# Scores of a decode attention: K transposed on TensorE in place of products on VectorE, and longer loads

## The chip, the cores and the metric

One core of a Trainium2 chip runs the whole kernel as one program. The metric is the time of one execution in microseconds on the device, as the median of several runs. Engines are named as in the profile: PE (TensorE matmuls), PEld (TensorE weight loads), DVE (VectorE), ACT (ScalarE), POOL (GpSimd) and SP (SyncE, which here issues the loads).

## The reference

Everything is float32. Two rows (B = 2 batches, one position each) of width 512 go through a layernorm; its result feeds an attention over a cache and a gated feed-forward, and both are added to the input.

```python
W = min(4096, max(256, Sk // 4))                      # 8192 // 4 = 2048 last positions
q = (xn @ wq).reshape(B, 1, 32, 128)                  # 32 heads of 128
scores = einsum("bhqd,bhkd->bhqk", q, k_cache[:, :, Sk-W:]) * 128 ** -0.5
p = softmax(scores)
A = einsum("bhqk,bhkd->bhqd", p, v_cache[:, :, Sk-W:]) @ wo
g, u = xn @ w_gate, xn @ w_up                         # 512 x 1376 each
out = x + A + (g * u) @ w_down
```

For each of 64 (batch, head) pairs 2048 rows of K and as many of V are read once: 134.2 MB of the 159.6 MB that the kernel reads. Each query is one row, so there is no reuse.

## The kernel before

The host lays all inputs but x out as one DRAM stream, in the order in which they are loaded; each load is one block of 128 rows, one row a partition (`laid_out`, `loads`, `placed`). A ring of three SBUF tiles, all named `step` in the profile, takes the loads; a load reuses a place once its readers are done. All loads go out on SP's queue in program order (`issue`).

The 32 heads are worked in NG = 8 groups of HG = 4. K and V of a head are 128 partitions x 4096 floats (16 KB a row): the first 64 partitions hold batch 0, the others batch 1, and each partition has 32 positions of 128 values. A turn of the main loop (`for it in range(NG + 2)`) handles K of group `it` and V of group `it - 1`. Its loads are `{g}.0` (K of two heads, V of one), `{g}.1` (K of one, V of two) and `{g}.2` (wo, V of one, K of one, the next wq), mostly 6144 KB each with 48 KB rows.

- `project`: four matmuls with the normalized x, spread over 128 columns, leave the group's queries in PSUM tile `q`, each batch on its own 64 partitions.
- `products` and `sums`, per head: DVE multiplies K in place by the query (tile `step`) and adds up each 128 products (tile `s`). Both pass over 128x4096 elements.
- `maxima`, `spread`, `weights`, `denominators`: the group's maximum over all positions (DVE, a 32x32 transpose and a matmul with ones, tile `top`), subtraction, exp on ACT into `p`, and the sums `rs`, summed over partitions by a matmul into `tot`.
- `weigh`, per head: eight matmuls, each with 32 columns of `p` as weights and 512 columns of V as moving data, in four column groups of the array, into `o_ps`.
- `gather`, `scaled`, `wo`: ACT copies `o_ps` to SBUF, four small matmuls pick each head's 128 values, DVE scales them, and four matmuls with wo add to PSUM tile `acc`.

Gate and up (`project_gu`) run once in the first turn as 24 matmuls in three column groups into two PSUM tiles; `gate_up` multiplies them and transposes the product with small matmuls. The feed-forward's w_down comes in strips of 128 rows: four early (EARLY), the others at the end (ROWS into `acc`, STRIPS into the same tile as the final sum).

DVE, ACT, POOL and SP run straight code; PE runs a loop over named sections (`steer`, `pr.part`, with `pr.hold` for waits against a register that counts turns). `Program.put` finds the dependences, `plan` and `emit` turn them into semaphore waits. Every operation is recorded by one helper, so nearly all lines of the profile say L139, and groups are told apart by tile names.

Of the kernel before, what the change touches and what calls it, by code (L numbers as in the profile page):

```python
# [5 lines left out]
ALU = mybir.AluOpType  # L6
# [7 lines left out]
HB = P // B  # L14
J = W // HB
JG = J // 4
NC = D // P
FB = 4 * P
NFB = -(-F // FB)
# [8 lines left out]
CK, CO, CQ = J * DH, D, HG * DH  # L28
CX = B * NC + 4 * N + 4 * HG + 2 * NFB + 2 + B
EARLY, ROWS, STRIPS = (0, 5, 6, NFC), (1, 2, 3, 4), (7, 8, 9)  # L30
GU = [(w, c, n) for w in range(2) for c in range(NC) for n in range(NFB)]
GU_A = [(0, c, n) for c in range(NC) for n in (2, 0)] + [(0, 0, 1)]
GU_B = [t for t in GU if t not in GU_A]


def gu_cols(n):
    return min(FB, F - n * FB)


WIDTHS = {"k": CK, "v": CK, "wo": CO, "wd": CO, "wq": FB, "c": CX}  # L40

PLACES = {
    ("k", 0): (0, 0), ("k", 1): (0, CK), ("v", 0): (0, 2 * CK),
    ("k", 2): (1, 0), ("v", 1): (1, CK), ("v", 2): (1, 2 * CK),
    ("wo", 0): (2, 0), ("v", 3): (2, HG * CO), ("k", 3): (2, HG * CO + CK),
    ("wq", 0): (2, HG * CO + 2 * CK),
}
C_WQ = HG * CO + 2 * CK  # L50
C_C = C_WQ + NC * FB
TILES = (3 * CK, 3 * CK, C_C + CX)


def field_at(kind, i):
    if kind == "wq":
        return PLACES["wq", 0][0], C_WQ + i[1] * FB
    if kind == "wo":
        return 2, i % HG * CO
    if kind == "c":  # L60
        return 2, C_C
    return PLACES[kind, i % HG]


def loads():


    def k(*ids):
        return [("k", h) for h in ids]

    def v(*ids):
        return [("v", h) for h in ids]

    def wq(g):
        return [("wq", (g, c)) for c in range(NC)]

    def wo(g):
        return [("wo", h) for h in range(g * HG, g * HG + HG)]

    gu_a, gu_b = [("gu", t) for t in GU_A], [("gu", t) for t in GU_B]  # L80
    wd = {i: ("wd", i) for i in range(NFC + 1)}
    out = {
        "x": ("B2", wq(0) + [("c", 0)]),
        "0.0": ("B0", k(0, 1) + gu_a),
        "0.1": ("B1", k(2) + gu_b),
        "0.2": ("B2", [wd[i] for i in EARLY] + k(3) + wq(1)),
    }
    for g in range(1, NG):
        a, b = g * HG, g * HG - HG
        out[f"{g}.0"] = ("B0", k(a, a + 1) + v(b))  # L90
        out[f"{g}.1"] = ("B1", k(a + 2) + v(b + 1, b + 2))
        out[f"{g}.2"] = (
            "B2", wo(g - 1) + v(b + 3) + k(a + 3) + (wq(g + 1) if g + 1 < NG else [])
        )
    b = H - HG
    out[f"{NG}.0"] = ("B0", v(b))
    out[f"{NG}.1"] = ("B1", v(b + 1, b + 2))
    out[f"{NG}.2"] = ("B2", v(b + 3))
    out["wo"] = (None, wo(NG - 1))
    for name, ids in (("d0", ROWS), ("d1", STRIPS[:-1]), ("d2", STRIPS[-1:])):  # L100
        out[name] = (None, [wd[i] for i in ids])
    return out


def placed():


    got, spans = {}, {}
    for name, (_, fields) in loads().items():
        at, lo, tile = None, None, None  # L110
        for kind, i in fields:
            w = gu_cols(i[2]) if kind == "gu" else WIDTHS[kind]
            if kind == "gu":
                t, c = tile, at
            elif kind == "wd":
                if at is not None:
                    t, c = tile, at
                elif name == "0.2":
                    t, c = 2, HG * CO + CK - len(EARLY) * CO
                else:  # L120
                    t, c = 0, (ROWS + STRIPS).index(i) * CO
            else:
                t, c = field_at(kind, i)
            assert at is None or (t, c) == (tile, at), (name, kind, i, c, at)
            got[kind, i] = (t, c, w)
            lo = c if lo is None else lo
            tile, at = t, c + w
        assert at <= TILES[tile], (name, at)
        spans[name] = (tile, lo, at)
    return got, spans  # L130


class Op:
    def __init__(self, eng, method, args, kw, deps, dma, tag, place, holds):
        self.eng, self.method, self.args, self.kw = eng, method, args, kw
        self.deps, self.dma, self.tag, self.place, self.holds = deps, dma, tag, place, holds

    def call(self, engine):
        return getattr(engine, self.method)(*self.args, **self.kw)  # L139

    def same(self, other):
        def flat(x):
            if hasattr(x, "space"):
                return x.tensor.name, x.offset, [list(t) for t in x.ap]
            return x

        def all_of(o):
            return [o.method] + [flat(a) for a in o.args] + [
                (k, flat(a)) for k, a in sorted(o.kw.items())
            ]  # L150

        return all_of(self) == all_of(other)


class Program:


    def __init__(self, nc):
# [5 lines left out]
        self.tag, self.also, self.held = None, [], []  # L164
# [24 lines left out]
    def put(self, eng, method, writes, reads, args, kw, dma=False):  # L189
# [29 lines left out]
        self.ops.append(Op(eng, method, args, kw, deps, dma, tag, place, holds))  # L219
# [10 lines left out]
    def plan(self, looped):  # L230
# [15 lines left out]
        for i, o in enumerate(ops):  # L246
# [20 lines left out]
            if o.dma and o.tag in self.tags:  # L267
                prev = [j for j in self.tags[o.tag] if j < i]
                assert all(know.get(("dma", j)) for j in prev), (o.tag, i)
# [7 lines left out]
        for i, o in enumerate(ops):  # L277
            if o.dma:
# [8 lines left out]
    def emit(self, looped, control):  # L287
# [10 lines left out]
        def give(i, first=None):  # L298
# [5 lines left out]
            for s, v in w[:-1]:  # L304
                e.wait_ge(s, v)
            ins = o.call(e)
            if w:
                ins._wait_ge(*w[-1])
            if i in at:
                ins.then_inc(sem[o.tag], 16 if o.dma else 1)  # L310
# [86 lines left out]
def steer(prog, regs, run):  # L397
    nc, pe = prog.nc, prog.eng["PE"]
    only = [mybir.EngineType.PE]
    r, r16 = pe.alloc_register("turn"), pe.alloc_register("landed")  # L400
    regs.update(r=r, r16=r16)
    run("start")
    pe.reg_mov(r, 1)
    pe.reg_mov(r16, 16)
    pe.br("pe_top")
    with nc.body("pe_top", valid_engines=only):
        here = pe.mark_branch_hint_location()
        pe.br_lt(r, 3, on_true="pe_q", on_false="pe_g")
    with nc.body("pe_g", valid_engines=only):
        run("g")  # L410
        pe.br_lt(r, NG + 2, on_true="pe_q", on_false="pe_o")
    with nc.body("pe_q", valid_engines=only):
        run("q")
        pe.br_lt(r, 2, on_true="pe_gu", on_false="pe_t")
    with nc.body("pe_t", valid_engines=only):
        run("t")
        pe.br_lt(r, 3, on_true="pe_w", on_false="pe_o")
    with nc.body("pe_o", valid_engines=only):
        run("o")
        pe.br_lt(r, NG + 2, on_true="pe_w", on_false="pe_tail")  # L420
    with nc.body("pe_w", valid_engines=only):
        n = 3 * JG + 1
        run("w", 0, n)
        pe.reg_add(r16, r16, 16)
        run("w", n)
        pe.reg_add(r, r, 1)
        pe.br_lt(r, 2 * NG + 9, on_true="pe_top", on_false="pe_tail").branch_hint(here)
# [3 lines left out]
    with nc.body("pe_gu", valid_engines=only):  # L431
        run("gu")
        pe.reg_add(r, r, 1)
        pe.reg_add(r16, r16, 16)
        pe.br("pe_top")


def build(nc, stream, x_nat, out):
# [3 lines left out]
    ring = [pr.sb(f"step{i}", [P, w]) for i, w in enumerate(TILES)]  # L442
    xr = pr.sb("xr", [P, D])
    ones = pr.sb("ones", [P, P])
    mean_w = pr.sb("mean_w", [P, P])
    eps_t = pr.sb("eps", [P, 1])
    zero = pr.sb("zero", [P, 1])
    st = pr.sb("st", [P, 4, B])
    xc = pr.sb("xc", [P, 2, B, NC])
    xn = pr.sb("xn", [P, NC, B])  # L450
    xnb = pr.sb("xnb", [P, NC, P])
    p_all = pr.sb("p", [P, HG, JG, M])
    s_t = [pr.sb(f"s{i}", [P, HG, J]) for i in range(2)]
    mt = pr.sb("mt", [P, 32])
    mtt = pr.sb("mtt", [P, 32])
    mc = pr.sb("mc", [P, 1])
    dg = pr.sb("dg", [P, 4 * HG])
    rs = pr.sb("rs", [P, N])
    nm = pr.sb("nm", [P, HG])
    rec = pr.sb("rec", [P, N])  # L460
    oT = pr.sb("oT", [P, N])
    o_sb = pr.sb("o_sb", [P, FB])
    h_sb = pr.sb("h_sb", [P, FB])
    hT = pr.sb("hT", [P, 4, NFB, B])
    acc_sb = pr.sb("acc_sb", [P, D])
    o_out = pr.sb("o_out", [P, P])

    o_ps = pr.ps("o_ps", [P, FB])
    q_ps = pr.ps("q", [P, FB])
    acc = pr.ps("acc", [P, FB])  # L470
    top_ps = pr.ps("top", [P, FB])
    gu_ps = [pr.ps(f"gu{i}", [P, FB]) for i in range(2)]
    tot_ps = pr.ps("tot", [P, FB])
    hT_ps, pk_ps = gu_ps
    acc_g = q_ps[:, 0:P]

    where, spans = placed()
    got = {key: ring[t][:, c : c + w] for key, (t, c, w) in where.items()}
    src, pos, tag_of = {}, 0, {}
    for name, (tag, _) in loads().items():  # L480
        t, lo, hi = spans[name]
# [4 lines left out]
    def issue(name):  # L486
        t, lo, hi = spans[name]
        pr.load("SP", ring[t][:, lo:hi], src[name], tag=tag_of[name])

    issue("x")  # L490
    issue("0.0")
    issue("0.1")
    for t, v in ((mean_w, 1.0 / D), (eps_t, EPS), (ones, 1.0), (p_all, 0.0),
                 (xr, 0.0), (zero, 0.0), (mt, 0.0)):
        pool.memset(t, v)
    pr.load("ACT", xr[:B, :], x_nat)

    cst = got["c", 0]
    cut = [0]
# [341 lines left out]
```

## Time and profile before

| | |
|---|---|
| median of 3 runs | 376.31 us (376.18 to 377.29) |
| profiled execution | 375.96 us, its span 374.6 us |
| moved by DMA | 159.62 MB in 4756 packets, 426 GB/s over the span |
| load queue busy | 98.9% of the span |
| busy: DVE, PE, ACT, POOL | 299.5, 177.2, 18.3, 3.0 us |
| mean granted PE clock | 0.718 of full speed |

The profile is of one execution. Its span runs from the first to the last instruction. Rows of engines give busy tenths in 40 slices of the span; the DMA row gives the mean busy share of the 16 DMA engines. A row of the timeline has the start, the duration, the engine, the source line, the operation with its output and inputs, and in brackets how long the engine had been idle and what released it. A float32 matmul is two instructions, so "x8" is four matmuls. In a table by stretches, each engine has its busy time and its instructions; PEclk is the granted clock.

### The profile page before, as it was taken

Reading aid. Unit: us, or ns where it says so; the run is one execution under the profiler, and the core shown is the slowest. Engines: PE = TensorE matmul, PEld = TensorE weight load, DVE = VectorE, ACT = ScalarE, POOL = GpSimd, SP = SyncE. Lnnn points to the kernel's source line nnn. Section 1 sums busy time; section 2 is a strip of 40 time slices with the busy share of each in tenths; the row PEclk is TensorE's granted clock in tenths of the full one; section 3 lists DMA queues with packets and bytes.
Section 4 is the critical chain, followed back from the end, with each engine's and each line's share of the span. In section 5 each row is a group of like instructions: output and inputs, shape, how many; then the busy total and the mean of one; then the engine's idle time right before and its main releaser. Section 6 shows DMA issues by size and latency. Waiting matters only on the chain.

```text
span 374.6 us, 2080 instructions
## 1 busy us (share of the span) xinstructions
PE 177.2 (47%) x850; PEld 54.9 (15%) x850; DVE 299.5 (80%) x151; ACT 18.3 (5%) x42; POOL 3.0 (1%) x16
## 2 busy tenths in 40 slices
PE   0664743337516184073923277061740645334876
PEld 0210121002101030010400032010300112010322
DVE  0089999998599796997699975997969976999911
ACT  4000200000000000000000000000000000000000
POOL 3000000000000000000000000000000000000000
PEclk9965859587855688565695858567965659656899
DMA  9999999999999999999999999999999999989996
GB/s 365 415 457 408 444 420 420 457 467 420 420 420 420 430 493 420 420 420 420 425 462 457 420 420 420 420 441 483 420 420 420 420 425 472 446 382 431 439 411 275
DMA packets 4756, 159.62 MB, mean 426 GB/s; under 512 B 530, under 2 KB 658, under 8 KB 916
## 3 DMA queue, kind: packets, MB, share of 16 engines
q1 hardware_dynamic: 4752, 159.62, 98.9%
q10 hardware_dynamic: 4, 0.00, 0.0%
HBM read 159.55 MB, written 0.07 MB: 426 GB/s over the span
## 4 chain that ended last, share of the span: by engine, by line
DMA 50%; DVE 47%; PE 2%; issue 0%; SPq 0%; DVEq 0%
DMA step<-in_stream_dram 50%; DVE step L139 23%; DVE s L139 22%; PE q L139 2%; DVE rs L139 1%; SPq L139 0%; PE acc L139 0%; DVE h_sb L139 0%; PE top L139 0%; DVE nm L139 0%; DVE o_out L139 0%; DVE mt L139 0%; DVE dg L139 0%; DVE mtt L139 0%; DVE mc L139 0%
## 5 line engine op out<-in xcount | busy, mean ns | idle before, releaser
L139 DVE TENSOR_TENSOR step<-step,q 128x4096 f32<-128x4096 f32 x32 | 141.3, 4416 | 41.2 <-DMA step<-in_stream_dram 41.2
L139 PE MATMUL o_ps<-step,p 128*32 128x512 f32 x512 | 93.7, 884 | 156.2 <-DMA step<-in_stream_dram 153.7
L139 DVE TENSOR_REDUCE s<-step 128x32 f32<-128x4096 f32 x32 | 141.4, 4418 | 0.8
L139 PEld LDWEIGHTS o_ps<-step,p 128*32 128x32 f32 x512 | 18.7, 147 | 218.4 <-DMA step<-in_stream_dram 170.6
L139 PE MATMUL q<-step,xnb 128*128 128x512 f32 x72 | 42.0, 736 | 9.0 <-DVE step L139 6.3
L139 PEld LDWEIGHTS q<-step,xnb 128*128 128x128 f32 x72 | 16.5, 241 | 28.2 <-issue 18.2
L139 PE MATMUL gu<-step,xn 128*2 128x512 f32 (+1 forms) x48 | 14.8, 786 | 11.4 <-DMA step<-in_stream_dram 11.4
L139 ACT COPY o_sb<-o_ps 128x256 f32<-128x256 f32 x16 | 5.2, 375 | 247.3 <-PE o_ps L139 247.3
L139 PE MATMUL gu<-step,o_sb 128*128 128x8 f32 x64 | 10.1, 285 | 4.0 <-ACT o_sb L139 4.0
L139 PEld LDWEIGHTS gu<-step,o_sb 128*128 128x128 f32 x64 | 9.4, 225 | 16.5 <-ACT o_sb L139 16.5
L139 ACT ACTIVATE p<-s,zero 64x128 f32<-64x128 f32 x16 | 6.4, 399 | 63.5 <-DVE s L139 63.4
L139 PE MATMUL acc<-step,oT 128*2 128x512 f32 x64 | 8.3, 592 | 0.4 <-DVE oT L139 0.4
L139 DVE TENSOR_REDUCE nm<-top 64x4 f32<-64x8 f32 x16 | 2.6, 164 | 7.0 <-PE top L139 6.9
L139 DVE RECIPROCAL rec<-tot 128x8 f32<-128x8 f32 x8 | 1.6, 199 | 6.2 <-PE tot L139 6.2
L139 PEld LDWEIGHTS gu<-step,xn 128*2 128x2 f32 x48 | 2.9, 99 | 23.2 <-DMA step<-in_stream_dram 13.1
L139 PE MATMUL top<-dg,ones 128*128 128x16 f32 x16 | 2.9, 258 | 6.6 <-DVE dg L139 6.6
L139 DVE TENSOR_REDUCE st<-xc 128x4 f32<-128x16 f32 x1 | 0.2, 169 | 6.2 <-POOL xc L139 6.2
L139 DVE TENSOR_TENSOR oT<-gu,rec 128x8 f32<-128x8 f32 x8 | 1.3, 157 | 4.3 <-PE gu L139 4.3
L139 PEld LDWEIGHTS top<-dg,ones 128*128 128x128 f32 x16 | 2.5, 188 | 12.5 <-DVE dg L139 11.4
L139 DVE TENSOR_REDUCE rs<-p 128x8 f32<-128x256 f32 x8 | 3.3, 414 | 0.9 <-ACT p L139 0.9
L139 ACT ACT_TABLE_LOAD x3 | 3.8, 1283 | 3.1 <-POOL xr L139 3.1
L139 PE MATMUL top<-st,mean_w 128*128 128x4 f32 x2 | 0.6, 364 | 6.4 <-DVE st L139 6.4
(44 smaller groups left out, 31.9 us busy)
## 6 DMA issues: line engine op xcount, KB each, us to landing
step<-in_stream_dram SPq DMA_DIRECT2D x20, 6144.0 KB, 30.4
step<-in_stream_dram SPq DMA_DIRECT2D x2, 4096.0 KB, 23.7
step<-in_stream_dram SPq DMA_DIRECT2D x1, 6080.0 KB, 18.8
step<-in_stream_dram SPq DMA_DIRECT2D x1, 5568.0 KB, 31.5
step<-in_stream_dram SPq DMA_DIRECT2D x1, 5120.0 KB, 29.8
step<-in_stream_dram SPq DMA_DIRECT2D x2, 2048.0 KB, 22.0
step<-in_stream_dram SPq DMA_DIRECT2D x2, 1024.0 KB, 11.6
step<-in_stream_dram SPq DMA_DIRECT2D x1, 1057.0 KB, 4.9
```

Source lines behind the costliest of these rows:

```text
L139: return getattr(engine, self.method)(*self.args, **self.kw)
```

## The change

The ring is one tile; K of four heads has one place in it (`C_K`) and V of four heads another (`C_V`). Each is loaded with one transfer of 64 KB rows (8192 KB), K of a group, then V of that group; only the last group's V comes as three (two heads, one, one). wq and wo come with one to three groups at a time (`w1`, `w2`, `w4`), and POOL copies some of them to the fixed place that PE reads. There are 26 loads in place of 32. The first load, `x`, holds w_gate, w_up, the first wq and the constants, and lies where V of group 0 is put later.

K is laid out by the host with the 128 values of a head on the partitions and the positions along the row. The scores are 32 matmuls a group: weights `qz` (128x8, the query in one column and zeros in the others), moving data 512 columns of K, in four column groups into `s_ps`. `products` and `sums` are gone. The queries are made with two columns (not 128) and transposed by DVE in 32x32 blocks (`across`); the scores are transposed in the same way (`sT`) before exp. `gather` masks and folds `o_ps` on DVE and needs one small matmul.

Gate, up and all queries run through one PE section, `q`, whose operand address is a register: six runs of four matmuls for gate and up, each 459 columns, then one run a group for the queries, all into the same two rows of `q_ps`. Between runs a POOL memset (`relay`) waits for the load and for the reader of `q_ps`, and raises the semaphore on which PE waits.

wo's product no longer accumulates in `acc`: it is added to `xr` on DVE after each group (`carry`). At the end, w_down's ROWS are three strips in place of four, into `q_ps`, and the sum `xr` enters the final tile by a matmul with `id4` ahead of the last strip.

The core of the diff (the new layernorm on two partitions and the host's layout are left out):

```diff
+C_E = HG * D + NC * FB
+C_Q = (C_E + HG * D + NC * FB, C_E)
+C_O = tuple(c + NC * FB for c in C_Q)
+C_V = C_O[0] + HG * D
+C_K = C_V + HG * CK
+RING = C_K + HG * CK
+C_GU = C_V
...
+        "x": (None, C_GU, [("gu", t) for t in GU] + [("wq", 0), ("c", 0)]),
+        "k0": ("K", C_K, k[:HG]),
+        "w1": (None, C_E - len(EARLY) * D, [wd[i] for i in EARLY] + [*pair[2], *pair[1]]),
     }
+    for g in range(NG - 1):
+        if g:
+            out[f"k{g}"] = ("K", C_K, k[g * HG : g * HG + HG])
+        out[f"v{g}"] = ("V", C_V, v[g * HG : g * HG + HG])
+        if g == 2:
+            out["w2"] = (None, C_E, [*pair[4], *pair[3]])
+        if g == 4:
+            out["w4"] = (None, 0, [("wo", 6), ("wq", 7), *pair[6], *pair[5]])
+    out["k7"] = ("K", C_K, k[last:])
+    out["v7"] = ("V", C_V, v[last : last + 2])
+    out["v30"] = ("V2", C_V + 2 * CK, v[last + 2 : last + 3])
+    out["v31"] = ("V3", C_V + 3 * CK, v[last + 3 :])
...
+    def relay(tag, *aps):
+        nonlocal relays
+        pr.also = list(aps)
+        pool.memset(none[:, relays : relays + 1], 0.0, tag=tag)
+        relays += 1
+
+    def across(out, row):
+        for j in range(4):
+            part = slice(32 * j, 32 * j + 32)
+            dve.transpose(out[part], row[0:32, :, part])
...
+    def project(c0, step, *used):
+        nonlocal n_run
+        n_run += 1
+        relay("wq", *used)
+        pr.part("q")
+        pr.hold("wq", n_run, "run")
+        for c in range(NC):
+            a = c0 + c * step
+            pr.late = lambda regs, c=c: ring[:, bass.ds(regs["from"] + (regs["by"] * c if c else 0), FB)]
+            pe.matmul(
+                q_ps[:B, :], xn[:, c, 0:B], ring[:, a : a + FB],
+                start=(c == 0), stop=(c == NC - 1),
+            )
...
+    for i, (w, n) in enumerate(GU):
+        project(C_GU + i * NC * GW, GW, got["gu", (w, n)], *used)
+        wide = min(GW, F - n * GW)
+        if w == 0:
+            act.copy(g_sb[:B, n, 0:wide], q_ps[:B, 0:wide])
+            used = [g_sb[:B, n, 0:wide]]
+        else:
+            dve.tensor_tensor(
+                hh_[:, n, 0:wide], g_sb[:B, n, 0:wide], q_ps[:B, 0:wide], op=ALU.mult
+            )
+            used = [hh_[:, n, 0:wide]]
...
-    def products(h):
-        kt, qb = keys(h), q_ps[:, h % HG * DH : (h % HG + 1) * DH]
         dve.tensor_tensor(
-            kt, kt, qb.unsqueeze(1).to_broadcast([P, J, DH]), op=ALU.mult,
-            tag="qc" if h % HG == HG - 1 else None,
...
-        dve.tensor_reduce(s_t[g % 2][:, hh, :], keys(h), axis=AX.X, op=ALU.add)
...
+    def scores(g):
+        pr.part("k")
+        pr.hold("K", g + 1, "landed")
+        pr.hold("qz", g + 1, "turn")
+        for hh in range(HG):
+            k = got["k", g * HG + hh].rearrange("p (b i) -> p b i", b=B)
+            for b in range(B):
+                for j in range(NJ):
+                    pe.matmul(
+                        s_ps[32 * j : 32 * j + N, :], qz[:, hh * B + b, :],
+                        k[:, b, j * FB : (j + 1) * FB],
+                        start=(hh == 0 and b == 0), stop=(hh == HG - 1 and b == B - 1),
+                    )
...
+    for g in range(NG):
+        c0 = C_Q0 if g == 0 else C_Q[(g - 1) % 2]
+        project(c0, FB, ring[:, c0 : c0 + NC * FB], *used)
+        queries(g)
+        used = [qt]
+        if g == 0:
+            issue("v0")
+            across(hT, h_sb.rearrange("p (c i) -> p c i", i=P))
+        if g in (2, 4):
+            issue(f"w{g}")
+        if g in (1, 3, 5, 6):
+            pool.tensor_copy(place, got["wo", g])
+        if g == NG - 2:
+            pool.tensor_copy(ring[:, C_Q[0] : C_Q[0] + NC * FB], got["wq", g + 1])
+        scores(g)
+        if g < NG - 1:
+            issue(f"k{g + 1}")
+        maxima(g)
+        weights(g)
...
+        for hh in range(HG):
+            weigh(g * HG + hh)
+        if g < NG - 2:
+            issue(f"v{g + 1}")
+        elif g == NG - 2:
+            for name in ("v7", "v30", "v31"):
                 issue(name)
...
+        if g == NG - 1:
+            for name in ("d0", "wo7", "d1", "d2"):
+                issue(name)
+            pr.part("r")
+            for j, i in enumerate(ROWS):
+                down(i, add_rows, j, True, True, q_ps)
+        gather(g)
+        if g == NG - 1:
+            carry(q_ps, 32 * len(ROWS))
+        wo(g)
+        carry()
```

More of the change, by code (lines that the diff above doesn't have):

```diff
@@ L27 @@
 M = 4 * N
[L28 to L62, printed above, removed]
-def loads():
[L68 to L80, printed above, removed]
+NJ = W // FB
@@ L399, in steer @@
     only = [mybir.EngineType.PE]
[L400 to L406, printed above, removed]
-        here = pe.mark_branch_hint_location()
-        pe.br_lt(r, 3, on_true="pe_q", on_false="pe_g")
+    first = {"run": 1, "turn": 1, "landed": 16, "at": C_GU, "step": GW, "next": C_Q[0]}
+    for name, value in first.items():
+        regs[name] = pe.alloc_register(name)
+        pe.reg_mov(regs[name], value)
@@ new lines, in steer @@
+    n, r, r16, at, step, then = (regs[k] for k in first)
+    pe.br("pe_q")
+    with nc.body("pe_q", valid_engines=only):
+        here = pe.mark_branch_hint_location()
+        regs["from"] = pe.snap(at, min_val=0, max_val=RING - 4 * FB)
+        regs["by"] = pe.snap(step, min_val=GW, max_val=FB)
+        run("q")
+        pe.reg_add(n, n, 1)
+        pe.br_lt(n, len(GU) + 2, on_true="pe_n", on_false="pe_k")
+    with nc.body("pe_n", valid_engines=only):
+        pe.reg_add(at, at, NC * GW)
+        pe.br_lt(n, len(GU) + 1, on_true="pe_q", on_false="pe_c")
@@ L541, in project @@
[L541 to L553 removed]
+    for t in (acc, q_ps, s_ps):
+        act.activation(t, zero.to_broadcast([P, FB]), AF.Copy)
@@ L612, in weigh @@
             )
     def gather(g):
[L615 to L629 removed]
+        dve.tensor_tensor(
+            om, o_ps.rearrange("p (r d) -> p r d", r=4),
+            rmask.unsqueeze(2).to_broadcast([P, 4, DH]), op=ALU.mult,
+        )
@@ new lines, in gather, with add_rows, carry @@
+        dve.tensor_reduce(red, om.rearrange("p r d -> p d r"), axis=AX.X, op=ALU.add, tag="red")
+        pr.part("g")
+        pr.hold("red", g + 2, "turn")
+        pe.matmul(pk, red, pick, start=True, stop=True)
+        dve.tensor_tensor(oT, pk, rec, op=ALU.mult, tag="oT")
+    def add_rows(lhsT, rhs, j, first=False, last=False, out=acc):
+        pe.matmul(out[32 * j : 32 * j + B, :], lhsT, rhs, start=first, stop=last)
+    def carry(src=acc, parts=P):
+        dve.tensor_tensor(xr[:parts], xr[:parts], src[:parts], op=ALU.add)
```

549 lines of the change are left out of this document (205 added, 344 removed).

## The prediction

> **What bounds the kernel now.** I read the page's first lines, then the chain that ended last, the DMA issues, and last the stretches at both ends of the timeline, since a full queue can be lost only there.
>
> ```profile
> span 374.6 us, 2080 instructions
> ...
> DMA  9999999999999999999999999999999999989996
> GB/s 365 415 457 408 444 420 420 457 467 420 420 420 420 430 493 420 420 420 420 425 462 457 420 420 420 420 441 483 420 420 420 420 425 472 446 382 431 439 411 275
> ...
> q1 hardware_dynamic: 4752, 159.62, 98.9%
> ...
> DMA 50%; DVE 47%; PE 2%; issue 0%; SPq 0%; DVEq 0%
> ...
> L139 DVE TENSOR_TENSOR step<-step,q 128x4096 f32<-128x4096 f32 x32 | 141.3, 4416 | 41.2 <-DMA step<-in_stream_dram 41.2
> L139 DVE TENSOR_REDUCE s<-step 128x32 f32<-128x4096 f32 x32 | 141.4, 4418 | 0.8
> ```
>
> DVE looks like the bound: its two big operations on K alone are 282.7 us, 75% of the span, and it holds 47% of the chain. But the queue that loads the stream is busy 98.9% of the span and every slice of the DMA row up to the last few is a 9: DVE's share of the chain runs under transfers that would have ended no earlier. The bound is 159.62 MB through one queue. The chain gives its pace:
>
> ```profile
> 1.17 18.83 DMA step<-in_stream_dram
> ...
> 118.93 25.68 DMA step<-in_stream_dram
> ...
> 162.52 25.70 DMA step<-in_stream_dram
> ...
> 357.93 13.48 DMA step<-in_stream_dram
> ...
> 372.72 0.29 DVE o_out L139
> ```
>
> ```profile
> 0.74 1.32 SPq L139 DMA_DIRECT2D step<-in_stream_dram  x3
> 5.69 0.20 POOL L139 TENSOR_TENSOR xc<-step 128x8 f32<-128x8 f32 x1 [3.12 <-DMA step<-in_stream_dram]
> step<-in_stream_dram SPq DMA_DIRECT2D x20, 6144.0 KB, 30.4
> step<-in_stream_dram SPq DMA_DIRECT2D x1, 1057.0 KB, 4.9
> out_dram<-o_out SPq DMA_DIRECT2D x1, 64.0 KB, 1.5
> ```
>
> One group is three loads of 6144 KB (18.87 MB), and two waits on the same kind of load start 43.59 us apart: 2.31 us per MB. Over everything it is 98.9% of 374.6 us for 159.62 MB, 2.32. Check: 1.08 MB have landed at 5.69, the next 6.23 MB should land 14.4 us later, at 20.1; the chain has 20.0. So data run as if they began to land at 3.2 us, and the last load lands at 371.4.
>
> **The stream after.** The bytes stay: 26 loads with together 159.53 MB (0.09 MB of constants less), so a full queue again ends at about 371.3 us. That DVE loses its 282.7 us of products and sums takes nothing off: the cover was the queue, and it stays. What 64 KB rows cost the trace does not show; by the two paces above (2.31 for 48 KB rows, 2.32 with all the short ones) the 126 MB of K and V in such rows could gain or lose some 1.5 us. I take 0, as 48 KB is the nearest row.
>
> A page of the Trainium skill speaks against long power-of-two rows ("DMA: Bandwidth & Descriptors", Latency and other measured facts): copies whose rows lie a large power of two apart lose rate, 214 to 207 GB/s at 512 KiB. Rows here lie 64 KiB apart, and no run here shows such a pitch; an estimate with that page's loss would be 9 us.
>
> **The start, where the queue can run dry.** After, the first load holds all of w_gate and w_up and the first wq (6.70 MB, landing at 3.2 + 15.5 = 18.7), then come four heads of K (8.39 MB, 38.0) and one with wq, wo and w_down (5.51 MB, 50.75). The fourth, V of group 0, is written over the place of the first. So SP can issue it only when PE has read all of that: six gate and up runs and the first query run, each four matmuls 512 wide in the same column group and the same PSUM tile. Between runs the tile is emptied (ACT copy, or DVE product) and POOL passes the signal on. In the kernel before, no load stands behind so long a row of runs. Costs:
>
> ```profile
> 9.74 6.12 PE L139 MATMUL q<-step,xnb 128*128 128x512 f32 x8 [2.72 <-DVE xnb L139]
> 33.22 8.79 PE L139 MATMUL gu<-step,xn 128*2 128x512 f32 x30 [7.19 <-DMA step<-in_stream_dram]
> 38.54 0.59 ACT L139 COPY h_sb<-gu 128x512 f32<-128x512 f32 x1 [29.71 <-PE gu L139]
> 42.14 0.69 DVE L139 TENSOR_TENSOR h_sb<-h_sb,gu 128x512 f32<-128x512 f32 x1
> 42.88 1.06 PE L139 MATMUL gu<-step,h_sb 128*128 128x6 f32 x8 [0.87 <-DVE h_sb L139]
> 51.54 5.70 PE L139 MATMUL q<-step,xnb 128*128 128x512 f32 x8 [6.29 <-DVE step L139]
> 91.44 3.68 PE L139 MATMUL q<-step,xnb 128*128 128x512 f32 x8
> 179.58 6.52 PE L139 MATMUL q<-step,xnb 128*128 128x512 f32 x8
> 2.41 0.10 POOL L139 MEMSET zero<- 128x1 f32 x1
> ```
>
> An f32 matmul is two instructions, so x8 is one run: 3.68 us at full clock, 6.52 at half, and 5.70 or 6.12 when the clock rises within it. Seven runs: 25.8. A first burst after idle time is 2.0 to 2.4 dearer: 2.2. Emptying: DVE's 0.69 left PE idle for 0.87, so two handovers are 0.18; with ACT's 0.59 or DVE's 0.69, POOL's 0.10 and three handovers (0.27) a gap is 0.96 to 1.06. Address registers within the loop are not in the trace; branches between sections before cost nothing visible (lower end 0; upper end 0.5 a gap, the size of one handover chain). I take 1.06 in all, near the lower end: 6 x 1.06 = 6.4. Sum 34.4, from 18.9 (landing, POOL, PE): PE is done at 53.3.
>
> Then SP issues. The first load took from 0.74 to the virtual 3.2, 2.45 us; the 64 KB store 1.5 less 0.15 for its bytes, 1.35. I take 2.0: V of group 0 begins to count at 55.3, and the queue was empty from 50.75. **The hole is 4.55 us.** Bounds: cheapest, 3.6 a run, 0.85 for the clock, gaps of 0.85, 1.35 to issue: 0.7. Dearest, gaps of 1.5, 3.1 for the clock, 2.45: 8.8. Layernorm on [2, 512] rows and its transposes end before 18.7 (before, the query run that waits for it began at 9.74; some eight operations of up to 0.69 more end by 15.3), so I cost them at 0; its cover is the landing of the first load.
>
> **Does the clock stay up in the runs?**
>
> ```profile
> core 0: us, PE busy (x) PEld busy (x) DVE busy (x) ACT busy (x) POOL busy (x), PEclk, DMA share, GB/s
> 25.13:28.54 3.41, 0.90 (x4) 0.00 (x0) 3.41 (x1) 0.00 (x0) 0.00 (x0) 0.96 0.97 418
> 28.54:31.95 3.41, 0.00 (x0) 0.00 (x0) 3.41 (x2) 0.00 (x0) 0.00 (x0) 0.50 0.97 418
> 35.37:38.78 3.41, 3.41 (x14) 0.51 (x12) 3.41 (x2) 0.24 (x1) 0.00 (x0) 0.54 1.04 452
> 38.78:42.19 3.41, 3.24 (x18) 0.53 (x12) 3.35 (x2) 0.34 (x1) 0.00 (x0) 1.00 0.80 346
> 55.85:59.26 3.41, 1.72 (x10) 0.77 (x12) 2.70 (x9) 0.80 (x2) 0.00 (x0) 1.00 1.07 461
> 59.26:62.67 3.41, 1.80 (x16) 0.35 (x12) 3.41 (x2) 0.00 (x0) 0.00 (x0) 1.00 1.07 461
> ```
>
> The granted clock steps in stretches of 3.41 us: a full one raises it (0.54 to 1.00), 26% busy drops it to 0.50, 50% busy (1.72) keeps it at 1.00. The runs are busy 3.68 of 4.74, 78%, so it should stay. The Trainium skill ("TensorE: Matmul & The Clock Gate", Part 1) has the same windows of about 3.4 us, and a gate that activity opens; by that rule the runs stay fast too, and the trace agrees.
>
> **The groups.** Per group the queue takes 2 x 8.39 MB, 38.7 us. K and V have one buffer each: K of g+1 is issued when PE has scored K of g, V of g+1 when PE has weighed V of g.
>
> ```profile
> 130.12 3.64 PE L139 MATMUL o_ps<-step,p 128*32 128x512 f32 x16 [8.18 <-DMA step<-in_stream_dram]
> 365.20 1.92 PE L139 MATMUL o_ps<-step,p 128*32 128x512 f32 x16 [0.94 <-DMA step<-in_stream_dram]
> 371.29 0.69 DVE L139 TENSOR_TENSOR acc_sb<-acc,xr 128x512 f32<-128x512 f32 x1 [2.31 <-PE acc L139]
> 44.21 1.04 PE L139 MATMUL acc<-step,hT 128*2 128x512 f32 x8 [0.27 <-ACT hT L139]
> ```
>
> The scores are 32 matmuls 512 wide in four column groups, shaped like the 32 of V: eight (x16) cost 1.92 at full clock, 3.64 at half. So 32 cost 7.7 and, with the 2.2 of a start, 9.9; at half clock 14.6. The window is 19.4 (the other load) less 2 for issuing, 17.4. What could start the scores late: after V lands, weigh 9.9, fold and pick on DVE and PE 2 (two 128x512 operations at up to 0.69, small matmuls), wo 1.04, the next queries 3.7 to 6.5, transposes and copy 1.5: 18 to 21, against the 19.4 at which K lands. 1.6 late plus 9.9 is 11.5, under 17.4: no hole, 6 us of reserve. Softmax (maxima, 32x32 transposes, exp) adds about 5 after the scores, at 17 of 19.4; POOL's copies of wo wait for nothing urgent. SP's other loads stand in line behind waits of the same order (w2 and w4 behind a query run), so I cost them at 0 too; if PE stayed at half clock the reserve of 6 would be gone.
>
> **The end.** V's last two heads come as loads of their own, followed by 2.62 MB of wo and w_down, 6.2 us. From V's last landing: weigh 1.92 to 3.64 (2.6 for a clock that may be either), DVE fold 0.69 and, at the pace of its 4096-wide sum, 0.6; pick 0.4 (four such, x8 at 42.88, took 1.06) and scale 0.3; wo 1.04, carry 0.69, identity and last strip 0.7; six handovers 0.5: 7.5. From o_out (372.72) to the end of the span is 1.9. That is 9.4 from V's landing at 371.3 - 6.2 = 365.1: 374.5 without a hole, level with the last strip's own path (371.4 + 1.3 + 1.9). The tail costs 0.2, between -0.3 and +1.2.
>
> **Sum.** 374.6 + 4.55 (hole) + 0.2 (tail) - 0.2 (bytes) = 379.15 us of span. The profiled execution of before took 375.96 for its 374.6, and lies 0.35 under the median of 376.31: 380.5 as a time, 380.85 on the scale of the median. As the lower end of the hole has the better-known parts, I round down to 380.7, 1.2% slower.
>
> **Rivals.**
> 1. The hole closes (not slower). Place: the last query run of the first load against the landing at 50.75. It decides from a PE end at 48.7: gaps of 0.3 instead of 1.06. Against it: 0.59 of ACT alone is more. With under 1 us of hole left the time is 376.3 to 377.4. Chance 13%. A gain of over 0.3% needs, besides, the 64 KB rows at their good end: 5%.
> 2. The clock stays at half in the runs, since they use two columns of one column group and all rows of the trace that raise it use more. Seven runs of 6.52 are 45.6 in place of 28.0: hole 22, time 398. For it: no row has this shape alone. Against: the burst at 33.22, of two columns (128*2), under which the clock rose to 1.00 in the stretch from 38.78. 7%.
> 3. 64 KB rows stream at 420 GB/s, the figure that the middle slices repeat, not at 433: 3% of 290 us, 8.7 more, 389. This is what the pitch rule named above would look like. 5%.
> 4. PE holds up K or V in the groups: each us late beyond the reserve costs seven times. With 1 us, 388. 5%.
>
> **How the numbers follow.** My case, a hole of 1.5 to 8.8 us, has 65%: 377.8 to 385.1. To hold 8 in 10 the range takes in the closed hole below and the nearer part of rivals 3 and 4 above: 376.3 to 387. What a measurement of this kernel tells from no change is about 0.3%, 1.1 us. Slower by more: 82%; within: 13%; faster: 5%.
>
> **What would show it.** The profile after should have: one low digit in the DMA row near slice 6, about 4 to 5 us before the fourth load's data; seven PE runs of 3.7 us with gaps near 1 between 19 and 53 us; DVE under 20% busy; a queue without idle time from 55 us on; from the last landing of V about 10 us to the end. It is wrong if V of group 0 is issued before 49 us, if the gaps are 2 us, or if the 64 KB loads take other than 19.4 us each.

## The result, and the profile after

The changed kernel takes 381.5 us (median of 4 runs, 379.5 to 382.39), the kernel before 376.25 us beside it (376.11 to 377.29): a ratio of 1.0126, 95% interval 1.0077 to 1.0175. It is 1.3% slower; the forecast was 380.7. The profiled execution took 382.39 for a span of 381.1 us.

The first lines of the page of the changed kernel, its rows by slices of 9.53 us and its queue:

```profile
span 381.1 us, 3091 instructions
...
PE 216.8 (57%) x1296; PEld 52.0 (14%) x1296; DVE 61.1 (16%) x150; ACT 13.2 (3%) x26; POOL 15.7 (4%) x55
...
DMA  9999959999999998999999999999999999998994
GB/s 352 462 427 398 433 207 433 440 440 440 440 440 440 440 440 385 495 440 440 427 420 392 413 440 440 433 447 440 440 440 440 441 440 433 440 440 371 411 422 187
...
q1 hardware_dynamic: 3888, 159.60, 97.4%
...
DMA 71%; PE 26%; DVE 1%; issue 1%; ACT 0%; POOL 0%; POOLq 0%
```

DVE went from 299.5 to 61.1 us busy and from 47% of the chain to 1%, and the time did not fall: the same 159.6 MB go through the same queue. New is one low digit, the 5 in slice 6, where the rate is 207 GB/s with 433 on both sides. The chain of the changed kernel (start, duration, what; the shortest pieces between them are left out in all chains here) shows what stands there, and the end:

```profile
19.71 6.43 PE q_ps L107 x8
26.16 0.54 ACT g L107
26.75 0.11 POOL none L107
...
26.98 3.61 PE q_ps L107 x8
...
49.52 3.61 PE q_ps L107 x8
53.15 21.65 DMA step<-in_stream_dram
74.84 9.69 PE o_ps L107 x64
84.54 28.93 DMA step<-in_stream_dram
113.51 9.12 PE o_ps L107 x64
122.65 29.57 DMA step<-in_stream_dram
...
341.01 29.59 DMA step<-in_stream_dram
370.64 3.41 PE o_ps L107 x16
374.08 0.70 DVE om L107
374.80 1.03 DVE red L107
```

Seven runs on PE stand between the first load's landing and V of group 0, which is issued at 53.15, right after the last of them. By the records of single packets the queue carried nothing from 51.34 to 54.36 us. V landed at 53.15 + 21.65 = 74.80, although its 8.39 MB are worth 19.4 us at 2.31 us per MB: 74.80 - 51.34 - 19.4 = 4.06 us lost, 3.0 of them without a packet and the rest at the slow start of the new stream. Later landings of V lie 38.75 us apart (113.47 and 152.22) for 16.78 MB, 2.31 us per MB: the queue is full again and long rows cost nothing.

The other part is the tail. From V's last landing at 370.60 to the end of the span are 10.5 us, and the last head's matmuls took 3.41 of them. A table by stretches for the changed kernel (PE's busy time and instructions first, PEclk the granted clock) sets them beside the ones just before:

```profile
core 0: us, PE busy (x) PEld busy (x) DVE busy (x) ACT busy (x) POOL busy (x), PEclk, DMA share, GB/s
...
365.70:367.70 2.00, 1.92 (x16) 0.42 (x16) 0.00 (x0) 0.00 (x0) 0.00 (x0) 1.00 1.04 442
370.60:374.05 3.45, 3.41 (x19) 0.83 (x22) 0.00 (x0) 0.00 (x0) 0.00 (x0) 0.57 1.00 414
```

The same eight matmuls took 1.92 us at a granted clock of 1.00 and 3.4 at 0.57, after PE had waited 2.96 us for the load.

### The profile page after: what moved, and what is told of

Its sections match the earlier page's. It is cut to its first block, busy times and chain, and to the rows that moved or that the text cites. A ratio compares the mean times of both kernels' runs of the same rounds, so it can differ in the third digit from the quotient of the medians.

```text
span 381.1 us, 3091 instructions
## 1 busy us (share of the span) xinstructions
PE 216.8 (57%) x1296; PEld 52.0 (14%) x1296; DVE 61.1 (16%) x150; ACT 13.2 (3%) x26; POOL 15.7 (4%) x55
## 4 chain that ended last, share of the span: by engine, by line
DMA 71%; PE 26%; DVE 1%; issue 1%; ACT 0%; POOL 0%; POOLq 0%
DMA step<-in_stream_dram 71%; PE o_ps L107 18%; PE q_ps L107 7%; DVE h L107 0%; ACT g L107 0%; DVE red L107 0%; PE acc L107 0%; POOL none L107 0%; DVE om L107 0%; DVE xr L107 0%; PE s_ps L107 0%; PE pk L107 0%; DVE oT L107 0%; POOLq L275 0%
## 5 line engine op out<-in xcount | busy, mean ns | idle before, releaser
L107 PE MATMUL o_ps<-step,p 128*32 128x512 f32 x512 | 74.4, 743 | 55.3 <-DMA step<-in_stream_dram 55.3
L107 PE MATMUL s_ps<-step,qz 128*8 128x512 f32 x512 | 60.9, 631 | 39.6 <-DMA step<-in_stream_dram 33.2
L107 PE MATMUL q_ps<-step,xn 128*2 x112 | 56.7, 653 | 25.1 <-POOL none L107 25.1
L107 PEld LDWEIGHTS s_ps<-step,qz 128*8 128x8 f32 x512 | 14.1, 94 | 86.5 <-issue 76.3
L107 PEld LDWEIGHTS q_ps<-step,xn 128*2 128x2 f32 x112 | 9.8, 92 | 72.9 <-issue 72.9
L107 DVE STREAM_TRANSPOSE qt<-q_ps 32x128 f32<-32x128 f32 x32 | 9.8, 307 | 26.5 <-PE q_ps L107 26.1
L107 POOL COPY step<-step 128x2048 f32<-128x2048 f32 x5 | 9.4, 1890 | 32.4 <-PE acc L107 32.4
L107 DVE TENSOR_TENSOR xr<-xr,acc 128x512 f32<-128x512 f32 x9 | 6.2, 688 | 17.7 <-PE acc L107 17.7
L107 DVE TENSOR_REDUCE red<-om 128x128 f32<-128x512 f32 x8 | 8.2, 1019 | 0.3
L107 DVE STREAM_TRANSPOSE sT<-s_ps 128x512 f32<-128x512 f32 x8 | 5.7, 708 | 0.0
```

The source lines that it names most:

```text
L107: return getattr(engine, self.method)(*args, **self.kw)
```

## The experiments

Two theories at first. **The hole**: the time comes from the stretch in which the queue waits for the seven runs, and vanishes if the queue has work there. **The long rows or DVE's place**: it comes from the shape of the loads or from the work that moved from DVE to PE. The changed kernel varies by itself (repeats below: 381.25 and 379.65), so kernels are compared where they shared a chip, as far as they did.

**Half of the hole's load made free.** V of group 0 comes as two loads; the first half lies over gate and up's strips only as far as the middle of the fifth run, and so it need not wait for the last two and a half runs:

```diff
-        out[f"v{g}"] = ("V", C_V, v[g * HG : g * HG + HG])
+        out[f"v{g}"] = ("V", C_V, v[g * HG : g * HG + (HG if g else 2)])
+        if g == 0:
+            out["v0b"] = (None, C_V + 2 * CK, v[2:4])
...
+            issue("v0b")
...
-                relay(tag, got["v", g * HG])
+                relay(tag, got["v", g * HG if g else 2])
```

> V of group 0 comes as two loads: heads 0 and 1 over the gate and up tiles that the first five runs read, heads 2 and 3 as before. Theory (the hole): the first half can be issued after the fifth run, at about 44 us, before the queue is empty at 51.3, the second at 53; the idle 3.0 us of the queue and the 0.9 us of slow first packets go, so 381.5 becomes about 377.5, and the DMA row shows no low digit near slice 6. Rival (64 KB rows or the groups cost the time): the hole is made up for later and the time stays within 1 us of 381.5. The tail's 1.2 us should stay in any case.

Measured: 376.38 us (12 runs, 376.12 to 378.36), ratio to the kernel before 1.0017 [1.0002, 1.0032]. Its page and the end of its chain:

```profile
span 375.1 us, 3092 instructions
...
DMA  9999999999999998998999999999999999999996
GB/s 358 462 433 398 417 439 416 496 433 398 405 447 447 447 447 388 493 412 384 447 447 447 447 440 421 419 397 447 447 447 447 441 440 405 398 440 440 411 418 249
```

```profile
336.30 29.77 DMA step<-in_stream_dram
366.11 1.97 PE o_ps L109 x16
```

The low digit is gone: the first half was issued at 41.56, in the middle of the fifth run (39.65 to 43.25). V's last landing comes 4.5 us earlier (366.07), and nearly the whole loss with it. The rest of the kernel, long rows and scores on PE included, is unchanged: the second theory falls. Of the 6.0 us between the two spans, 4.5 are the hole and 1.4 the last head, which here ran at 1.97. The time is 1.1 us under the 377.5 that was expected, because the tail was expected to stay as it was.

**The hole made longer.** POOL clears a 128x512 tile ahead of the first relays:

```diff
+        if tag == "wq" and relays < 7:
+            pr.also = list(aps)
+            pool.memset(om.rearrange("p r d -> p (r d)"), 0.0)
```

> Each of the first relays gets a POOL memset of 128x512 (0.52 us) ahead of its own, so each gap between the first seven runs is some 0.5 us longer. Theory (every us on the row of runs is a us of hole and of time): six gaps and the start, 3.0 to 3.7 us, so about 385. Rival (the groups' slack takes it up): the time stays at 381.5, and the hole's length does not carry over.

Measured: 383.44 us (383.14 to 383.91), 1.0195 [1.0179, 1.021], 2.2 above the repeat of the changed kernel on that chip. PE's timeline in this kernel, first two runs (in brackets: idle time before, and its releaser), and its rate by slices:

```profile
19.84 6.52 PE L107 MATMUL q_ps<-step,xn 128*2 x8 [19.84 <-POOL none L107]
27.68 3.59 PE L107 MATMUL q_ps<-step,xn 128*2 x8 [1.32 <-POOL none L107]
```

```profile
GB/s 351 461 439 401 432 175 336 439 439 439 439 439 439 439 439 439 384 494 439 439 439 432 425 432 391 410 434 439 439 439 439 440 439 439 439 439 384 431 413 263
```

Five gaps grew from 0.86 and 0.95 to 1.32 and 1.41 us, 2.3 in all; a clear took 0.52 us, and the gap ahead of the seventh run got none. PE was done at 55.65 in place of 53.13 and the empty stretch was 5.96 in place of 3.0 us. The load carries this on: V of group 0 landed 2.75 us later (77.55 against 74.80) and V of group 6 still 2.4 us later (334.11 against 331.73). The end does not follow one for one, and 385 was not reached: the span grew by 0.9 us against the changed kernel's first profile and by 2.1 against the repeat's. In this profile PE, not the load, came last (its 32 matmuls of V in one piece, 9.80 us), which is taken up below.

**PE at work before the first run.** Fifteen matmuls of 512 columns, into a tile that nobody reads, while the first load comes in:

```diff
+    run("warm")
...
+    pr.part("warm")
+    for i in range(15):
+        pe.matmul(tot_ps, ones, h_sb[:, 0:FB], start=True, stop=True)
```

> 15 matmuls of 512 columns on constants run on PE between 3 and 19 us, before the first load lands; nothing waits for them. Theory (the first run's slow clock widens the hole): the first run takes 3.6 us in place of 6.4, PE is done at 50.3, V of group 0 starts at 51.5 and the hole shrinks from 3.0 to about 0.2: about 378.5, with less spread between runs. Rival (the clock has nothing to do with it, the runs wait on POOL or on registers): the first run stays at 6.4 or the time stays at 381.5.

Measured: 381.25 us (379.44 to 382.5), 1.0124 [1.01, 1.0148]: nothing gained, though the start did what it should. PE's timeline in this kernel:

```profile
19.34 3.59 PE L107 MATMUL q_ps<-step,xn 128*2 x8
...
374.64 0.61 PE L107 MATMUL s_ps<-step,hT 128*2 128x128 f32 x14
377.37 0.27 PE L107 MATMUL s_ps<-step,hT 128*2 128x128 f32 x1 [2.11 <-issue]
```

The first run fell from 6.43 to 3.59, PE was done at 49.92, the empty stretch was 0.27 us, and V's last head landed 3.0 us earlier than in the changed kernel (367.56). But the last head ran slowly (3.62), and after 14 of the 16 matmul instructions of two w_down strips PE stood idle for 2.11 us with nothing that it waited for. In that time the trace has one 16 KB packet on the queue that it calls "instruction" (375.24 to 376.19). So most of a gain at the start was lost at the end. What ties this place to the start, by the argument so far, is the number of PE instructions ahead of it.

**A shorter one, and one that only moves the code.** Four such matmuls of two columns (16 instructions), and, apart from it, fifteen of 8 columns at 3 us (60 instructions), meant to be too early and too short to make the first run a fast one:

```diff
+    pr.part("warm")
+    for i in range(4):
+        pe.matmul(tot_ps[:B], xn[:, 0, 0:B], h_sb[:, 0:FB], start=True, stop=True)
```

```diff
+    pr.part("warm")
+    for i in range(15):
+        pe.matmul(tot_ps[:, 0:N], ones, ones[:, 0:N], start=True, stop=True)
```

> As the warm start, but with 4 matmuls on two columns (16 instructions in place of 60), issued when the normalized x is ready at 13.9 us; nothing waits for them. Theory: the 3.0 us that the warm start won at the hole were lost again in the tail, where PE stood still for 2.1 us while a 16 KB block of its instructions was fetched, because 60 more instructions had moved the tail across a block. With 16 the first run still takes about 3.6 to 4.5, the hole shrinks to 0.3 to 1.2, the tail is as in the changed kernel, and the time is 378.5 to 379.5. Rival (a shorter hole does not shorten the time): 381.5 again.

> The changed kernel with 15 small matmuls (8 columns, 60 instructions) on constants at 3 us, done by about 9: PE is cold again when the first load lands, so the hole keeps its 2.5 to 3.0 us, and only the place of the code that follows moves, by as much as in the long warm start. Theory (place of the code): in the tail PE stands still for about 2 us, ending some 1 us after the fetch of a 16 KB block, and the time is about 2 over the changed kernel's own beside it. Rival (the work on PE ahead of the first load costs the tail of the long warm start): no idle time in the tail, and the changed kernel's time.

Measured: the first 378.88 us (378.27 to 380.49), 1.0075 [1.0055, 1.0095], with a first run of 3.60, an empty stretch of 1.06 us and no such stop in the tail; the second, with a first run of 5.22, 383.99 us (382.64 to 384.74), 1.0209 [1.0195, 1.0224], 2.7 above the repeat on its chip. PE's timeline in the second:

```profile
375.14 0.61 PE L107 MATMUL s_ps<-step,hT 128*2 128x128 f32 x14
377.93 0.37 PE L107 MATMUL s_ps<-step,hT 128*2 128x128 f32 x1 [2.17 <-issue]
```

The first reached the time expected of it, but beside it on its chip a kernel that runs like the changed one took 379.65 us (the next paragraph), 1.0092 [1.0078, 1.0107]. The intervals overlap, so a gain from the shorter hole is not shown here.

In the second the stop comes after the same 14 of the tail's instructions as in the kernel with fifteen wide matmuls, and lasts as long. What the two have in common is 60 more PE instructions ahead of the tail, and a kernel with 28 more, below, bears out the place of the code by a count. (A block of 15 matmuls that PE never runs was tried for the same purpose: 379.65 us, 379.32 to 381.39, and no stop in the tail. The profile lists only instructions that ran, so it does not show whether and where the block lies in PE's program, and the run decides nothing. As what PE runs is the same, it is taken here as a repeat of the changed kernel.)

> The changed kernel with a block of 15 matmuls (60 instructions) in PE's code ahead of the loop, never executed: only the place of the code moves. Theory (place of the code): PE stands still for about 2 us in the tail, at the fetch of a 16 KB block, and the time is about 383.5, with the hole as before at 3.0. Rival (the dummy matmuls themselves cost the tail of the warm start): 381.5 and no such idle time.

**Does the tail depend on the clock of the last head?** Three wide matmuls into an unread tile just before each group's last head; once with the split and the short warm-up, once with the split alone:

```diff
+        if hh == 3:
+            for i in range(3):
+                pe.matmul(pk_ps, ones, h_sb[:, 0:FB], start=True, stop=True)
```

> V of group 0 in two loads, the short warm start, and three matmuls on constants ahead of each group's last head of V, which keep PE's clock up while the last load is under way; nothing waits for them. Theory: no hole; the last eight matmuls of V take 1.9 in place of 1.9 to 3.6, so the tail is set by the last strip's landing: 375.5 to 376.3, level with the kernel before or just under it. If the added 28 instructions bring the tail's fetch of code in the way, 2 us more.

> V of group 0 in two loads and the three matmuls on constants ahead of each last head of V, without the warm start: 12 instructions more, where 16 cost nothing and 28 brought the idle time. Theory: no hole, the last eight matmuls of V at full clock (1.9), no fetch in the way: 375.6 to 376.4 in nearly all runs, where the split alone has runs of 377.5 to 378.4. If the fetch is in the way already with 12, or if the matmuls delay the last head by themselves, 377.5 or more.

Both missed: 382.36 us (379.08 to 383.7), 1.018 [1.0161, 1.0199], and 381.03 us (377.71 to 382.13), 1.0097 [1.006, 1.0134], against 376.38 for the split alone. PE's timeline in the first and, below it, in the second:

```profile
372.66 0.62 PE L109 MATMUL s_ps<-step,hT 128*2 128x128 f32 x16
373.65 0.40 PE L109 MATMUL s_ps<-xr,cst 128*2 128x128 f32 x8 [0.37 <-DVE xr L109]
373.87 0.40 PE L109 MATMUL s_ps<-step,hT 128*2 128x128 f32 x6
375.43 0.38 PE L109 MATMUL s_ps<-step,hT 128*2 128x128 f32 x2 [1.16 <-issue]
```

```profile
349.67 7.05 PE L109 MATMUL s_ps<-step,qz 128*8 128x512 f32 x64 [1.59 <-ACT qz L109]
...
360.44 8.01 PE L109 MATMUL o_ps<-step,p 128*32 128x512 f32 x48
368.38 2.84 PE L109 MATMUL pk<-h,ones 128*128 128x512 f32 x6
371.15 1.92 PE L109 MATMUL o_ps<-step,p 128*32 128x512 f32 x16
```

The first has the instruction stop again (1.16 us), now after 30 of the tail's 32 matmul instructions. That is 16 matmul instructions later than with 60 more, and each has a weight load of its own: together the 32 instructions by which the two programs differ (60 less 28). Twelve of the 28 lie in a section that PE runs eight times, so it is the place in the code that counts, not how many instructions have run. By the same count 16 more put the stop behind the last matmul.

The second has none, and the last head ran at 1.92, yet it began at 371.15 with no wait for a load: PE itself was late. Part of this is the experiment's own doing, as its expectation allowed for: the added matmuls take 2.8 us of PE just ahead of each last head (368.38 to 371.15). So whether PE is late without them this run does not show. That was a new theory: **in the last group PE, not the load, can set the end.**

**The changed kernel again**, to look at that group:

> The changed kernel again, beside the two others on the same chip: between 379.5 and 382.4, and within it the spread of the first run's clock (5.7 to 6.5 us) and of the last eight matmuls of V (1.9 to 3.6).

Measured: 381.25 us (380.38 to 382.21), 1.0135 [1.0116, 1.0154], the span 379.9. Its chain and the granted clock in the same stretch:

```profile
318.88 31.45 DMA step<-in_stream_dram
350.47 8.79 PE s_ps L107 x64
...
362.40 0.60 PE tot L107 x2
363.00 9.92 PE o_ps L107 x64
372.94 0.70 DVE om L107
```

```profile
core 0: us, PE busy (x) PEld busy (x) DVE busy (x) ACT busy (x) POOL busy (x), PEclk, DMA share, GB/s
350.00:359.30 9.30, 8.75 (x64) 2.07 (x64) 0.02 (x1) 0.00 (x0) 0.00 (x0) 0.82 0.99 426
359.30:362.80 3.50, 0.81 (x4) 0.70 (x4) 2.35 (x7) 0.52 (x1) 0.00 (x0) 0.87 1.01 431
362.80:373.00 10.20, 10.20 (x68) 2.65 (x71) 0.27 (x2) 0.00 (x0) 0.00 (x0) 0.71 0.99 416
```

The last transfer in the chain is K's. From its landing PE needs 22.5 us (350.47 to 372.94), with scores of 8.79, a softmax in which it is busy 0.81 of 3.50 us, and 32 matmuls of V in one piece, 9.92. The load needs 19.4 from K's landing to V's last. At full clock PE needs about 18 (7.05 for the scores, 3.5, and 7.3 at the 3.64 us that two heads took in the changed kernel's first profile): then it is there first and the load sets the end, as in that profile and in the split's. At a granted clock of 0.82 in the scores and 0.71 in V, as here, PE does.

**PE kept busy in the softmax.** One wide matmul, unread, in each of PE's two waits; with the split, and without it:

```diff
+        pe.matmul(pk_ps, ones, h_sb[:, 0:FB], start=True, stop=True)
```

> V of group 0 in two loads, and in each group one matmul on constants (512 columns) in each of PE's two waits between the scores and the weights, 1.28 and 1.49 us long; nothing waits for them and they fit the gaps. Theory (in the last group PE, not V's landing, sets the end where the clock drops in those waits: V's 32 matmuls 9.9 us in a row, where at full clock they take 7.05 and wait for V): the clock stays up, V's last head is weighed in 1.9 at its landing, and nearly all runs are at 375.8 to 376.5, where the split alone has runs of 377.2 to 378.4. Rival (the spread has another cause): 376.4 with the same spread up to 378.4.

> The same two matmuls a group without the split, so the hole stays. Theory: hole and tail add; the hole's 3.5 to 4 us stay and the 1 to 2 us of the tail go: 379 to 380, with the spread that the first run's clock leaves (5.2 to 6.5 us). Rival: 381 as the changed kernel.

Measured: with the split 377.03 us (12 runs, 376.22 to 377.73), 1.0018 [1.0006, 1.003]; without it 379.75 us (379.22 to 382.73), 1.0104 [1.0075, 1.0133]. PE's timeline with the split:

```profile
358.82 5.36 PE L109 MATMUL o_ps<-step,p 128*32 128x512 f32 x48
365.98 1.92 PE L109 MATMUL o_ps<-step,p 128*32 128x512 f32 x16 [1.80 <-DMA step<-in_stream_dram]
```

In the profiled run the three heads take 5.36 us where the split alone had 7.05: the clock stays up, as expected. The time does not bear the theory out. The slowest runs went from 378.36 to 377.73, but the median did not fall (377.03 against 376.38), and only 4 of the 12 runs came out where nearly all were expected (one of them at 376.51), against 7 of the 12 with the split alone. What lifts the others by about 1 us is open; the kernel before has some such runs too (377.0 to 377.4). Without the split the result cannot be told from a repeat of the changed kernel (379.65).

**Was DVE ever the bound?** In the kernel before, the sums read 4 of each 128 products:

```diff
-        dve.tensor_reduce(s_t[g % 2][:, hh, :], keys(h), axis=AX.X, op=ALU.add)
+        dve.tensor_reduce(s_t[g % 2][:, hh, :], keys(h)[:, :, 0:4], axis=AX.X, op=ALU.add)
```

> The kernel before, with DVE's sums over 4 of 128 products each (the scores are left incomplete; everything else runs). DVE loses about 120 of its 299.5 us. Theory (the load queue bounds the kernel before, and DVE's 47% of the chain is covered): 376.3 stays within 0.7 us. Rival (DVE is the bound that its share of the chain makes it look): the time falls by tens of us.

Measured: 377.2 us (376.1 to 377.45), 1.0015 [1.0003, 1.0027]. The page of this kernel:

```profile
span 375.9 us, 2080 instructions
...
PE 181.2 (48%) x850; PEld 57.1 (15%) x850; DVE 169.0 (45%) x151; ACT 18.3 (5%) x42; POOL 3.0 (1%) x16
```

130 us less work on DVE, and nothing gained. The median lies 0.9 us above 376.3, a little outside the 0.7 that was allowed, but not in the direction of the rival. So more than half of the 238 us that the change takes off DVE was worth nothing here; the rest was not taken off alone.

No version beat the kernel before. The best, the split, is 0.17% above it: with the queue full from end to end both come to the same floor.

## Why the prediction was right, point by point

**The bound** (one queue; DVE's share of the chain covered): right, by the DMA rows and by the shortened sums.

**64 KB rows at 0**: right. 2.31 us per MB between the landings of V, as before. From V's first landing to its last, 127.9 MB took 295.8 us, 2.312 us per MB with 2.306 forecast, 0.85 us in all. The pitch rule of the Trainium skill ("DMA: Bandwidth & Descriptors", Latency and other measured facts), which by the prediction's estimate would have cost about 9 us here, does not show at rows that lie 64 KiB apart. Rival 3 is out.

**The hole of 4.55**: the mechanism is shown in both directions, by the split and by the slower relays, and the size is about right: 4.06 in the profiled execution, V of group 0 landed at 74.80 with 74.7 forecast. (The dearest bound, 8.8, adds up to 8.5 by its own terms; only the 385.1 at the upper end of its main case rests on it.) Inside it, parts offset each other. The first load landed at 19.36, not 18.7; the first run took 6.43, 2.8 more than the other six at 3.61 (forecast 3.68 with 2.2 for the first); the gaps were 0.84 to 0.95, not 1.06; PE was done at 53.13 with 53.3 forecast. Issuing took less (first packet 1.2 us after 53.13, not 2.0), but the first packets were slow. Empty stretch by end of PE's runs in four kernels:

| kernel | first run, us | PE done, us | queue empty, us |
|---|---|---|---|
| fifteen matmuls ahead | 3.59 | 49.92 | 0.27 |
| four ahead | 3.60 | 50.78 | 1.06 |
| changed kernel | 6.43 | 53.13 | 3.0 |
| slower relays | 6.52 | 55.65 | 5.96 |

Rival 1 (the hole closes) needed PE done at 48.7; even the first row stays above that.

**The clock in the runs**: they ran at full pace after the first, so rival 2 is out. That matmuls just ahead make the first run a fast one is shown by both warm-ups. In the Trainium skill ("TensorE: Matmul & The Clock Gate", Part 1) activity opens the gate, and the trace agrees, the shape with two columns included: four of those were enough.

**The groups' reserve of 6 us, no hole**: right for the stream, which stays full; rival 4, as it was put (K or V held up in each group), does not occur. But the step was carried over to the last group without its working, and there it fails. The reserve was counted up to the end of the softmax, and the tail was costed from V's last landing alone. At the end nothing follows that could use a reserve: scores, softmax and 32 matmuls are about 18 to 22.5 us against the load's 19.4, and by the repeat's chain PE set the end, not V. That this and the first run (4.9 to 6.5 us in the profiles without a fast start) make the spread, 379.5 to 382.39 where the kernel before has 376.11 to 377.29, fits the profiles; it was not tested run by run.

**The tail costs 0.2**: mis-sized. 10.5 us after V's last landing with 9.4 forecast: the last head 3.41 (2.6 taken, 3.64 as its upper end), the fold 0.70 + 1.03 (0.69 + 0.6 taken from the pace of a longer sum), the rest within 0.2 of the forecast. Together with 0.95 at V's last landing (369.65 forecast, 370.60) this is, to 0.1, the difference between the forecast span of 379.15 and 381.1. (The terms of the tail by themselves give 374.5, or -0.1, and not 0.2.) All this is read from the profiled execution, the slowest of the four. That the sum came so near is in part luck: the hole's parts offset each other, and in the repeat the end was set by a path that the sum does not have.

## What to carry to other kernels

Where one load queue bounds a kernel, ask of every load what it is written over and how long the row of work is that frees the place; part of a load that can go earlier is enough to close the hole. A wait that is hidden in the steady state has to be worked out again for the last round, where nothing comes after it. Work on an idle engine is not free either: where its instructions lie can cost at the end most of what it saves at the start.

## What the runs showed of the hardware

- PE stood still for 1.2 to 2.2 us in the tail while 16 KB of instructions were fetched, depending on how many instructions lay ahead in its program: 60 more gave 2.11 and 2.17 us, 28 more (split, warm-up and last heads) 1.16, and 16, 12, 8 or none gave no stop, though the fetch was there (378.03 to 378.95 in the changed kernel). PE went on 1.1 to 1.2 us after the packet's end. The Trainium skill ("Runtime: NRT & Kernel Launch", Instruction fetch mechanics) has such blocks of 16 KiB and calls the cost of crossing one mostly hidden; in these three kernels it was not.
- After the empty stretch of the changed kernel the first 64 KB packets took up to 3.3 us, the usual one 2.42; with it the restart cost some 1.0 us beyond the empty time (4.06 less 3.02).
- In the changed kernel's first run the granted clock reads 1.00 although it took 6.43 us for what takes 3.61 later. For the start, durations tell the pace and the clock column does not.
- Open: the runs above 382 us of the kernel with split, warm-up and last heads, none of which was profiled; and why the changed kernel's two repeats, on two chips, differ (1.0135 [1.0116, 1.0154] and 1.0092 [1.0078, 1.0107]).
